# The last pair of row blocks: one sum turned, added and stored in two halves of rows

## The chip, the cores and the metric

The kernel runs on one core of a Trainium2 chip. Its time is the device time of one execution in microseconds (us); the figure of a kernel is the median of its runs. Five engines work side by side, each with its own queue: TensorE (PE in the profile; its weight loads are PEld), VectorE (DVE), ScalarE (ACT), GpSimd (POOL) and SyncE (SP), which only issues transfers. ScalarE issues transfers too (ACTq).

## The reference, cut to what matters

```
xn = layernorm(x)                              # x: 2048 rows, 640 columns
a, b = xn @ Wd_re.T, xn @ Wd_im.T              # DFT along the columns
y = Ws_re @ a - Ws_im @ b                      # DFT along the rows, real part
h = gelu(xn @ w1 + b1)                         # 640 -> 1536
out = x + y + (h @ w2 + b2)                    # 1536 -> 640
```

All inputs and the output are float32.

## The kernel before, in words

TensorE multiplies numbers split into a high and a low part, three matmuls for one product (`product`, `split`). First comes the GELU branch for four blocks of 512 rows, with x added; its results wait in DRAM (`ys`). Then the two Fourier products follow, the second as a fast product of seven multiplications, in which sums of operands replace multiplications.

The work after the GELU branch is a list of entries (w, u): w is one of the seven multiplications, u a part of it. Each entry has a *form*, an operand of TensorE in two halves: `form(n)` lets ScalarE write the high half (line 159) and VectorE the low half (line 160). The main loop goes through the entries in order. At entry n it emits TensorE's matmuls (`sequence_entry`, `hidden_entry`), then the functions listed as `pre` for that step, then `form(n + 3)`, then those listed as `post` (lines 1234 to 1238). So the lists fix VectorE's order by hand: what stands in `pre` runs ahead of the form, what stands in `post` behind it. Engines start their instructions in that order, and an instruction waits until the data that it needs is there and the place that it writes is free.

The stages named "y" (`hidden_beside`, `hidden_entry`) finish a pair of row blocks, ta and tb, over the hidden columns: 21 entries, w from 0 to 6 and u from 0 to 2. The results gather in PSUM banks. X, Y and Z stand for pairs of banks of 512 columns each (`banks[:, X : X + 2]` is `x_`), US and VS for single ones. A multiplication with w over 2 goes on in banks that an earlier one has begun. X is written by w = 0, 3, 5 and 6, and its contents are needed as they stand after w = 5, for block tb, and after w = 6, for block ta.

In the last pair (`last` is true), the matmuls of entries 18 to 20 (w = 6) are emitted at entries 18 and 19: at 18 first 15 into VS, which use the forms 18, 19 and 20 in turn, then 15 into bank X, and at 19 15 into bank X + 1 (from line 1188 on). These are TensorE's last 45 matmuls.

Step 17 is the one ahead of these. Its `pre` holds `add(v1, v1, x_)` on VectorE, then comes the last form, `form(20)`, and then `yb2, yb2`: the first call turns v1 in blocks of 32x32 (`turned`, line 839), the second adds what was turned to the columns 64 to 127 of each quarter of block tb (`columns(1)`, a tile that holds what the GELU branch left and was loaded into u2) and stores them (`out_b`, `store`). `add` is recorded as line 407, all issues of `store` as line 817. `store` issues four transfers, one for each quarter of the partitions; with `both` the first two go to SyncE's queue and the last two to ScalarE's. Step 18 does the same for VS (y4). After the loop, X is turned, added and stored (yt_2), and X + 1 in two halves of eight of the sixteen groups of rows (lines 1246 to 1257; yt_last).

A transfer signals its end through one of eight counters that the transfers of both queues take in rotation.

Of the kernel before, what the change touches and what calls it, by code (L numbers as in the profile page):

```python
# [17 lines left out]
B = 32  # L18
# [7 lines left out]
def kernel(  # L26
# [38 lines left out]
    nc = tc.nc  # L65
    x = x.flatten_outer_dims()
# [5 lines left out]
    NB = TB // B  # L72
# [32 lines left out]
    def bank(k):  # L105
        return banks[:, k]
# [62 lines left out]
    def rows_of(ap, t):  # L169
        return ap[t * TB : (t + 1) * TB].rearrange("(n r) d -> r n d", r=B)  # L170
# [108 lines left out]
    def hidden(g):  # L279
        i = g % NF  # L280
        acc = bank(g % 3)
        kinds = ((0, 0), (0, 1), (1, 0))
        steps = [(j, k) for j in range(ND) for k in range(3)]
        if g == 0:

            steps.sort(key=lambda s: s[1] == 1)
        for n, (j, k) in enumerate(steps):
            a, b = kinds[k]
            nc.tensor.matmul(  # L289
                acc, W1[i][:, a, j * P : (j + 1) * P], XT[j][:, b], start=n == 0, stop=n == len(steps) - 1  # L290
            )
        return acc
# [40 lines left out]
    A = {}  # L333
# [72 lines left out]
    def add(dst, a, b, op=ALU.add):  # L406
        nc.vector.tensor_tensor(dst, a, b, op=op)  # L407
# [23 lines left out]
    def load_a(g):  # L431

        for f in steps_of_load(g):
            f()
# [71 lines left out]
    def f5(u):  # L506
        add(held("ci1", u), held("ci1", u), held("ci2", u))

    def f6(u):
        add(held("cr1", u), held("cr1", u), held("ci1", u))  # L510
# [121 lines left out]
    last = NC - 1  # L632
# [91 lines left out]
    for g in range(NG):  # L724
# [9 lines left out]
        if i == NF - 1:  # L734
            acc = hidden(g + 2) if g + 2 < NG else None
# [19 lines left out]
        else:  # L755
            acc = hidden(g + 2)
# [42 lines left out]
    def load_part(t, k):  # L799
        nc.sync.dma_start(new_sum(1, t, k), part_of(t, k))  # L800

    def gather(h, t, k, acc, first=False, op=ALU.add):

        if h == 0 and first:
            nc.scalar.activation(new_sum(h, t, k), acc, AF.Copy, scale=-1.0 if op == ALU.subtract else 1.0)
        else:
            add(sums[t, k], sums[t, k], acc, op)
# [6 lines left out]
    def store(t, src, c0, c1, both=False, n0=0, n1=NB):  # L814

        for q in range(Q):
            (nc.scalar if both and q > 1 else nc.sync).dma_start(
                rows_of(out, t)[:, n0:n1, q * DQ + c0 : q * DQ + c1], src[q * B : (q + 1) * B, n0:n1]
            )
# [12 lines left out]
    def turned(acc, name):  # L832

        if len(acc.shape) == 2:
            yt = A["yt"](name)[:, 0]
            nc.vector.transpose(yt, acc)
        else:
            yt = A["yt"](name)
            nc.vector.transpose(yt.rearrange("p e n -> p (e n)"), acc.rearrange("p e n -> p (e n)"))
        return yt  # L840

    def add_turned(dst, yt):
        if len(yt.shape) == 2:
            add(dst, dst, yt.rearrange("p (n i) -> p n i", i=B))
        else:
            d = dst.rearrange("p n (e i) -> p e n i", i=B)
            add(d, d, yt.rearrange("p e (n i) -> p e n i", i=B))
# [182 lines left out]
    def load_g(b, i):  # L1030
        if i >= NW * ND:
            return
        w, c = G[i]
        n = GWIDE[w] * P
        places = A["g", b]
        k = i % len(places)
        if b < len(blocks) - 1 and w == NW - 1:

            k = (i - 2) % len(places)
            if c in CHUNKS[0]:  # L1040
                k = CHUNKS[0].index(c)
                places = {k: fr_tile((P, 6 * P), f"u{2 - k}_{sets[blocks[b]]}", f"gr{k}_{b}", F32R)}
        g = places[k][:, : 2 * n].rearrange("p (a b) -> p a b", a=2)
        GT[b, i] = g
        nc.sync.dma_start(g.bitcast(F32), wits[w][c])

    def hidden_beside(b, n):


        ta, tb = blocks[b - 1][1], blocks[b][1]  # L1050
        last = b == len(blocks) - 1
        x_, y_, z_ = (banks[:, k : k + 2] for k in (X, Y, Z))
        us, vs = bank(US), bank(VS)
        ya = yo[ta]

        def s(which, k):
            return sums[(ta, tb)[which], k]

        def t2(k):
            return lambda: add(s(1, KU[k]), s(1, KV[k]), s(1, KU[k]), ALU.subtract)  # L1060

        def t3(k):
            return lambda: add(s(0, KU[k]), s(1, KU[k]), s(0, KU[k]), ALU.subtract)

        def t4(k):
            return lambda: add(s(0, KV[k]), s(0, KV[k]), s(1, KU[k]), ALU.subtract)

        def columns(k):

            return s(1 if last else 0, ("u1", "u2")[k]).rearrange("p a b -> p (a b)").rearrange("p (n e) -> p n e", n=NB)  # L1070

        def load_yb(k):
            return lambda: nc.sync.dma_start(columns(k), ys[k][tb])

        def copy(dst, src):
            return lambda: nc.scalar.activation(dst, src, AF.Copy)

        def to(dst, acc, name, then=lambda: None):


            def f():
                add_turned(dst, turned(acc, name))
                then()

            return f

        def out_a(c0, c1):
            return lambda: store(ta, ya[:, :, c0:c1], c0, c1) if last else None

        def odd():  # L1090
            yt = turned(us, f"yo_{tb}")
            add_turned(ya[:, :, 4 * B :], yt)
            add_turned(yo[tb, 4], yt)
            out_a(4 * B, DQ)()

        def in_two(k):

            acc, name = s(1, ("v2", "v1")[k]), f"yb{k}_{tb}"

            def f():  # L1100
                if name not in A:
                    A[name] = turned(acc, name)
                else:
                    add_turned(columns(k), A.pop(name))
                    out_b(k)()

            return f

        def out_b(k):
            return lambda: store(tb, columns(k), 2 * k * B, 2 * (k + 1) * B, last and k == 1)  # L1110

        yb1, yb2 = in_two(0), in_two(1)
        yb4 = to(yo[tb, 4], vs, f"yb4_{tb}", lambda: store(tb, yo[tb, 4], 4 * B, DQ, last))
        f5s = [lambda u=u: f5(u) for u in range(2)] if not last else [lambda: None] * 2
        f6s = [lambda u=u: f6(u) for u in range(2)] if not last else [lambda: None] * 2
        pre = {
            17: [lambda: add(s(1, "v1"), s(1, "v1"), x_)],
        }.get(n, [])
        post = {

            0: [lambda: gather(1, tb, "v1", z_), lambda: gather(1, tb, "v", vs, op=ALU.subtract), f5s[0]],
            1: [f5s[1]],
            3: [to(ya[:, :, : 2 * B], x_, f"ya1_{ta}")],
            4: [t2(0)],
            5: [t2(1)],
            6: [to(ya[:, :, : 2 * B], y_, f"ya2_{ta}", out_a(0, 2 * B)), t2(2)],
            7: [odd],
            8: [t3(0)],
            9: [copy(s(1, "v1"), z_), t3(1)],
            10: [t3(2)],  # L1130
            11: [t4(0)],
            12: [copy(s(1, "v2"), x_), t4(1)],
            13: [load_yb(0), t4(2), load_yb(1)] if last else [t4(2)],
            14: [lambda: add(s(1, "v2"), s(1, "v2"), z_), yb1],
            15: [yb1] if last else [load_yb(0)],
            16: [] if last else [load_yb(1)],
            17: [yb2, yb2] if last else [yb1, yb2],
            18: [yb4] if last else [yb2],
            19: [f6s[0]],
            20: [] if last else [f6s[1], yb4],  # L1140
        }.get(n, [])
        if not last:
            if n in (12, 13):
                post.insert(0, lambda: load_g(b, (NW - 1) * ND + 13 - n))
            if n == 18:
                post[:0] = [lambda k=k: load_part(blocks[b + 1][1], k) for k in ("u1", "u")]
            if n == 20:
                post.append(lambda: load_a(put_off[0]))

                def end():  # L1150
                    to(ya[:, :, 2 * B : 4 * B], x_, f"ya3_{ta}")()
                    store(ta, ya, 0, DQ)

                later.append(end)
        return pre, post
# [91 lines left out]
    y = yo[t]  # L1247
    add_turned(y[:, :, 2 * B : 3 * B], turned(bank(X), "yt_2"))
    store(t, y[:, :, 2 * B : 3 * B], 2 * B, 3 * B, True)
    yt = A["yt"]("yt_last")[:, 0].rearrange("p (n i) -> p n i", i=B)  # L1250
    d, a = y[:, :, 3 * B : 4 * B], bank(X + 1).rearrange("p (n i) -> p n i", i=B)
# [36 lines left out]
```

## Time and profile before

| what | us |
|---|---|
| median of 3 runs | 862.92 (862.8 to 864.06) |
| the profiled execution | 862.76 |
| its span, first to last instruction | 861.0 |
| TensorE busy | 851.5 |
| VectorE busy | 623.4 |
| last matmul begins | 854.12 |
| last operation of VectorE ends | 856.27 |

The span starts at 0. The profile's timeline gives, for each instruction, its start, its duration, its engine, its line in the kernel, the tiles written and read, and in brackets how long the engine had been idle before it and what ended the wait. The view of waits sums these by who waited for whom. A transfer has an issue (the time on the queue that issues it) and a landing.

### The profile page before, as it was taken

The numbers are of one execution on the slowest core, as the hardware profiler recorded it, in microseconds if no ns is written. First come the engines' busy times: TensorE is split into PE (matmuls) and PEld (weight loads), VectorE is DVE, ScalarE is ACT, GpSimd is POOL, SyncE is SP. The second block draws the span as 40 slices with busy tenths as digits, with TensorE's granted clock in tenths as the row PEclk, the third lists the DMA queues.
The fourth block names the chain that finished last, engine by engine and source line by source line (L and its number), as shares of the span: only waits on it lengthen the run. The fifth ranks groups of instructions, "written<-read, shape, count | busy, mean of one in ns | idle before, by whom it ended". The sixth has DMA issues, their size and how long they took to land.

```text
span 861.0 us, 10245 instructions
## 1 busy us (share of the span) xinstructions
PE 851.5 (99%) x3754; PEld 703.4 (82%) x3754; DVE 623.4 (72%) x792; ACT 333.1 (39%) x460; POOL 21.0 (2%) x22
## 2 busy tenths in 40 slices
PE   8999999999999999999999999999999999999996
PEld 6888888888888888888888888888888888888885
DVE  6554555366443678989989787998977988885596
ACT  5454434245333555443434334232322423222241
POOL 0000300030003000000000000000000000000000
PEclk9999999999999999999999999999999999999999
DMA  6747476875566984938753659853765779704464
GB/s 180 226 134 180 89 183 182 215 157 174 155 164 152 321 357 88 221 103 213 173 145 86 184 172 278 209 132 101 196 175 167 257 181 230 304 19 177 126 186 86
DMA packets 208689, 152.34 MB, mean 177 GB/s; under 512 B 82432, under 2 KB 183040, under 8 KB 208128
## 3 DMA queue, kind: packets, MB, share of 16 engines
q1 hardware_dynamic: 195728, 137.93, 61.7%
q10 hardware_dynamic: 12912, 13.77, 4.6%
q8 instruction: 29, 0.48, 0.2%
q14 instruction: 20, 0.16, 0.1%
HBM read 108.67 MB, written 42.99 MB: 176 GB/s over the span
## 4 chain that ended last, share of the span: by engine, by line
PE 98%; DVE 1%; DMA 0%; ACT 0%; issue 0%
PE banks L272 26%; PE banks L273 26%; PE banks L271 26%; PE banks L289 19%; DMA x<-in_A_x_dram 0%; DVE st L184 0%; PE banks L627 0%; DVE yo L407 0%; DVE mv L185 0%; DVE yt_last L1254 0%; DVE xp L207 0%; ACT xt L159 0%; ACT mv L191 0%; DVE mv L193 0%; DVE mv L196 0%
## 5 line engine op out<-in xcount | busy, mean ns | idle before, releaser
L272 PE MATMUL banks<-as,xab 128*128 128x512 f32 x407 | 158.5, 389 | 0.0
L271 PE MATMUL banks<-as,xab 128*128 128x512 f32 x407 | 158.3, 389 | 0.0
L273 PE MATMUL banks<-as,xab 128*128 128x512 f32 x407 | 158.3, 389 | 0.0
L159 ACT ACTIVATE as<-r 128x1024 fp32r<-128x1024 f32 x80 | 85.0, 1062 | 173.6 <-PE banks L273 148.8
L160 DVE TENSOR_TENSOR as<-r,as 128x1024 fp32r<-128x1024 f32 x80 | 97.2, 1216 | 39.3 <-ACT as L159 39.3
L289 PE MATMUL banks<-xt,xab 128*128 128x512 f32 x420 | 99.2, 390 | 0.2 <-ACT xt L159 0.2
L304 DVE TENSOR_TENSOR hs<-ab,hs 128x512 fp32r<-128x512 f32 x48 | 36.5, 760 | 84.2 <-ACT hs L302 84.2
L289 PEld LDWEIGHTS banks<-xt,xab 128*128 128x128 f32 x420 | 78.4, 188 | 17.3 <-ACT xt L159 1.3
L272 PEld LDWEIGHTS banks<-as,xab 128*128 128x128 f32 x407 | 76.4, 188 | 16.5 <-DVE as L160 0.5
L271 PEld LDWEIGHTS banks<-as,xab 128*128 128x128 f32 x407 | 76.4, 188 | 15.9
L273 PEld LDWEIGHTS banks<-as,xab 128*128 128x128 f32 x407 | 76.4, 188 | 15.6
L271 PE MATMUL banks<-as,xc 128*128 128x512 f32 x224 | 87.1, 389 | 0.0
L272 PE MATMUL banks<-as,xc 128*128 128x512 f32 x224 | 87.1, 389 | 0.0
L273 PE MATMUL banks<-as,xc 128*128 128x512 f32 x224 | 87.1, 389 | 0.0
L298 ACT ACTIVATE ab<-banks,b1c 128x512 f32<-128x512 f32 x48 | 33.0, 688 | 100.6 <-PE banks L289 97.7
L159 ACT ACTIVATE as<-rt 128x1024 fp32r<-128x1024 f32 x32 | 34.0, 1062 | 70.1 <-PE banks L273 57.9
L289 PE MATMUL banks<-xt,as 128*128 128x512 f32 x240 | 57.0, 389 | 0.0
L289 PEld LDWEIGHTS banks<-xt,as 128*128 128x128 f32 x240 | 45.0, 188 | 9.4
L272 PEld LDWEIGHTS banks<-as,xc 128*128 128x128 f32 x224 | 42.0, 188 | 8.8
L271 PEld LDWEIGHTS banks<-as,xc 128*128 128x128 f32 x224 | 42.0, 188 | 8.8
L273 PEld LDWEIGHTS banks<-as,xc 128*128 128x128 f32 x224 | 42.0, 188 | 8.6
L271 PE MATMUL banks<-hs,xc 128*128 128x512 f32 x120 | 46.7, 389 | 0.0
(161 smaller groups left out, 1364.3 us busy)
## 6 DMA issues: line engine op xcount, KB each, us to landing
raw<-in_A_dft_seq_re_dram SPq DMA_DIRECT2D x64, 256.0 KB, 5.6
raw<-in_A_dft_seq_im_dram SPq DMA_DIRECT2D x64, 256.0 KB, 5.2
wit<-wst ACTq DMA_DIRECT2D x20, 384.0 KB, 3.5
ws<-wit SPq DMA_DIRECT2D x15, 384.0 KB, 5.2
xs<-x SPq DMA_DIRECT2D x64, 80.0 KB, 1.8
xo<-in_A_x_dram SPq DMA_DIRECT2D x16, 320.0 KB, 6.1
forms_ab<-xab SPq DMA_DIRECT2D x4, 1280.0 KB, 5.8
xab<-wit SPq DMA_DIRECT2D x13, 384.0 KB, 4.8
```

Of the source, the lines that this page charges most:

```text
L159: nc.scalar.activation(h, s, AF.Copy)
L160: nc.vector.tensor_tensor(l, s, h.bitcast(F32), op=ALU.subtract)
L271: nc.tensor.matmul(acc, wh, mh, start=first, stop=False, skip_group_check=goes_on)
L272: nc.tensor.matmul(acc, wh, ml, start=False, stop=False, skip_group_check=goes_on)
L273: nc.tensor.matmul(acc, wl, mh, start=False, stop=last, skip_group_check=goes_on)
L289: nc.tensor.matmul(acc, W1[i][:, a, j * P : (j + 1) * P], XT[j][:, b], start=n == 0, stop=n == len(steps) - 1)
L298: nc.scalar.activation(a, acc, AF.Gelu_apprx_tanh, bias=b1c[:, i : i + 1])
L304: nc.vector.tensor_tensor(hs[:, 1], a, hs[:, 0].bitcast(F32), op=ALU.subtract)
```

## The change

In the last pair, step 17 has no addition ahead of the last form any more. Behind the form, in place of the two calls of `yb2`, stands one new function, `by_halves`. For rows 0 to 7 of the sixteen groups, and then for rows 8 to 15, it adds the half of `x_` to the half of v1, turns that half, adds it to the half of `columns(1)`, and stores the half through both queues. `out_b` still serves the other stores, and its last argument is dropped. The other pair of row blocks keeps its order.

```diff
         def out_b(k):
-            return lambda: store(tb, columns(k), 2 * k * B, 2 * (k + 1) * B, last and k == 1)
+            return lambda: store(tb, columns(k), 2 * k * B, 2 * (k + 1) * B)
+
+        def by_halves():
+
+            acc, yt, d = s(1, "v1"), A["yt"](f"yb1_{tb}"), columns(1)
+            for n0 in (0, NB // 2):
+                n1 = n0 + NB // 2
+                a, x, y = (v[:, :, n0 * B : n1 * B] for v in (acc, x_, yt))
+                add(a, a, x)
+                nc.vector.transpose(y, a)
+                add_turned(d[:, n0:n1], y)
+                store(tb, d, 2 * B, 4 * B, True, n0, n1)
 
...
         pre = {
-            17: [lambda: add(s(1, "v1"), s(1, "v1"), x_)],
+            17: [] if last else [lambda: add(s(1, "v1"), s(1, "v1"), x_)],
         }.get(n, [])
...
-            17: [yb2, yb2] if last else [yb1, yb2],
+            17: [by_halves] if last else [yb1, yb2],
```

## The prediction

> **What bounds the kernel now.** First the page's table of engines (part 1) and its chain of work that ended last (part 4):
>
> ```profile
> PE 851.5 (99%) x3754; PEld 703.4 (82%) x3754; DVE 623.4 (72%) x792; ACT 333.1 (39%) x460; POOL 21.0 (2%) x22
> PE 98%; DVE 1%; DMA 0%; ACT 0%; issue 0%
> ```
>
> TensorE is busy for 99% of the span and makes up 98% of the chain. So an edit outside TensorE counts in two ways only: it makes TensorE wait or stop waiting, or it moves what follows TensorE's last matmul. The change touches VectorE's order and the stores at the very end, so I read two stretches of the timeline. The first is around the step that is edited, all engines (start, duration, engine, line, what it does):
>
> ```profile
> 845.06 1.22 DVE L407 TENSOR_TENSOR v<-v,banks 128x1024 f32<-128x1024 f32 x1
> ...
> 846.19 0.69 DVE L160 TENSOR_TENSOR as<-v,as 128x512 fp32r<-128x512 f32 x1
> ...
> 846.52 0.39 PE L271 MATMUL banks<-as,xab 128*128 128x512 f32 x1
> 846.79 1.24 DVE L839 STREAM_TRANSPOSE yb<-v 128x1024 f32<-128x1024 f32 x1
> 846.93 0.19 PEld L272 LDWEIGHTS banks<-as,xab 128*128 128x128 f32 x1 [0.45 <-DVE as L160]
> 846.93 0.50 PE L272 MATMUL banks<-as,xab 128*128 128x512 f32 x1
> ...
> 847.27 0.40 PE L273 MATMUL banks<-as,xab 128*128 128x512 f32 x1
> ...
> 847.50 0.40 PE L271 MATMUL banks<-as,xab 128*128 128x512 f32 x1
> ...
> 848.07 1.23 DVE L407 TENSOR_TENSOR u<-u,yb 128x1024 f32<-128x1024 f32 x1
> ```
>
> The first row is the full-width addition that step 17 runs ahead of the last form; the L160 row is the low half of that form; the transpose and the last row are yb2. The matmul at 846.93 is the first that needs the low half (ended 846.88). Matmuls start 0.227 us apart elsewhere, so it was due at 846.75: a wait of 0.19 us, then one spacing of 0.34 and ten that sum to about 0.05 too much. Eleven spacings on, TensorE is **0.34 us** late. No other VectorE wait holds TensorE after 840 us.
>
> The second stretch is the end, from the timelines of VectorE, ScalarE's queue and SyncE's queue, and the waits of SyncE's queue (total, times, longest):
>
> ```profile
> 855.85 0.43 DVE L407 TENSOR_TENSOR yo<-yo,yt_last 128x256 f32<-128x256 f32 x1
> ```
> ```profile
> 855.49 1.88 ACTq L817 DMA_DIRECT2D out_dram<-yo  x4
> ```
> ```profile
> 857.13 1.82 SPq L817 DMA_DIRECT2D out_dram<-yo  x4
> ```
> ```profile
> SPq L817 <- DMA out_dram<-yo: 2.7, 3, 1.4
> ```
>
> ScalarE issues its four last stores from 855.49, as soon as the data is there. SyncE issues its own four only from 857.13, since each transfer also waits for an earlier transfer to land. The trace's records of the transfers show why: each raises one of eight counters, taken in rotation through one list of the transfers of both queues, and waits until the transfer eight places earlier has landed. In the last part of the list ScalarE's stores stand ahead of SyncE's. SyncE's first store of the last half-block waits for ScalarE's store issued at 855.49, which lands 1.6 us later.
>
> **The change, part by part.** Times are those of the profiled execution: 862.76 us, of which 861.0 are the span and 1.76 lie around it; it is 0.16 under the median of 862.92, so the sum can stand beside the median.
>
> *The addition leaves its place ahead of the last form.* The L160 row moves from 846.19 to 845.06 (ScalarE's high half ended at 844.63) and ends at 845.75, ahead of the matmul due at 846.75. The wait goes: minus 0.34.
>
> *What is late next.* `by_halves` issues six operations in this order: add, turn, add turned for rows 0 to 7, then the same for rows 8 to 15. The two additions named `add(a, a, x)` read the banks X and X+1. Entry 18 (line 1192) first fills bank VS with 15 matmuls, and then writes X, starting over the same columns that the additions read. Before, one addition had read X by 846.28, over a microsecond before the first matmul into X (847.50, or 847.20 without the wait above). Now X is free only after the second half's addition, and that is fifth in VectorE's queue behind the low half. Durations: additions of 128x512 take 0.69, and start 0.60 after the one before when they need not wait for it (846.19 to 846.79); a transpose of 128x512 takes 0.72; an operation that needs the one before starts 0.03 after its end (848.07 against 846.79 + 1.24). So:
>
> - low half 845.06 to 845.75; first add 845.66 to 846.35; transpose 846.38 to 847.10; add of the turned half 847.13 to 847.82; second add 847.73 to **848.42**.
> - First matmul into X: 0.05 after that (846.88 to 846.93), at 848.47, instead of 847.20. Wait 1.27, and the 0.15 that the restart cost above (0.34 less 0.19): plus **1.42**.
>
> TensorE's end therefore moves by 1.42 − 0.34 = **+1.08**, from 854.51 to 855.59. The wait is not in the trace of before; its lower end is 0 (the additions released early, or the second half of the bank not protected) and its upper end 2.9, if all six operations had to end (849.89) ahead of X. I take 1.42, since only the two additions read X. Behind the waiting matmul stand 29 more, which all move with it, and behind these the last transposes. VectorE's other work is covered: its six halves end at 849.89 instead of 849.30, y4 then ends at about 851.4, and X is ready for the next transpose only at 852.2.
>
> The page "VectorE: DVE Perf Modes" of the Trainium skill, section "The DRAIN you can't avoid", says that the next operation does not start until the pipe of the one before is empty, except for those that need not be held. The rows show starts 0.09 us ahead of the end before; by the strict reading the second add would end at 848.69 and the forecast be 0.27 higher.
>
> *The stores.* Two stores of four transfers replace one: SyncE and ScalarE each issue two more, of 64 KB instead of 128. An issue takes 0.32 to 0.5 us, ScalarE has nothing else to do there, and SyncE's last ones come after the TensorE end anyway. What counts is whom the last SyncE transfers wait for. I carry the rotation on by hand: each queue's transfers are listed in the pace at which the list of before has them, half as long for 64 KB. Then SyncE's second store of the half X (the one named yt_2) falls eight behind ScalarE's first store of the last half-block, and four transfers stand behind it; before, it was the next one, with three behind it. With everything 1.08 later: ScalarE's store is issued at 856.57, has landed by 858.2, and five SyncE issues follow at 0.45 each (1.82 for four): the last at 860.0, landed 1.65 later (these stores' medians are 1.6 and 1.7). Before, the last was issued at 858.5. So the tail adds **+0.45**. Ends: the gate one place further back, 0; one or two places ahead, +0.9 or +1.35; no gate at all, about −2.2 (last add at 857.36, two issues, landing at 859.45 instead of 861.67).
>
> Sum: 862.76 + 1.08 + 0.45 = **864.3 us**.
>
> **Rivals.**
>
> - *No new wait, the old one gone.* If X were free in time (both additions run first, or nothing ties the second to X), TensorE gains 0.34: 862.4, or 862.9 with the tail's 0.45. Against it: the written order, and that bank X is continued, not started anew. 10%.
> - *The stores' queue, slower than forecast and slower than before.* The place is SyncE's queue after 857; it decides if ScalarE's store that is late stands eight ahead of a SyncE transfer with six or more instead of four behind it: 0.45 for each, so 865.2 to 865.6. For it: ScalarE gets two more transfers ahead and SyncE already lags 2 us. 17%.
> - *The rotation falls well.* SyncE's last stores then wait for nothing late: 864.3 − 2.2 = 862.1 with the new wait; near 860.6 only if the new wait fails to come too. 6%, of which 2 for the latter.
> - *The clock.* The longer wait could lower TensorE's granted clock. The nearest row is the stretch after TensorE stops, with a clock of 0.73; 30 matmuls at 0.227 would take 9.3 instead of 6.8 us: 866.8. The clock stayed at 1.00 through the old wait. 3%. The Trainium skill's page "TensorE: Matmul & The Clock Gate", section "HAM oscillation — how this bites in real kernels", names idle gaps over about 3.4 us as the cause; no run here has a gap of 1.3 us to show it.
>
> **How the numbers follow.** The forecast has 64%, between 863.4 and 864.9. A measurement of this kernel can tell about 0.2%, or 1.7 us: faster means below 861.2, slower above 864.65. Of the forecast's 64 some 14 lie above 864.65. Slower: 14 + 17 + 3 = 34%. Faster: the 2% where the rotation falls well and the wait does not come, and one more for what I overlook: 3%. Within 0.2%: 63%. The range takes the forecast, most of the first rival and of the stores' queue: 862.2 to 865.5.
>
> **What would show it.** In the profile after: the L160 row of 128x512 at about 845.1 and no wait of TensorE for it; a TensorE wait of 1.2 to 1.3 us near 847.2, put down to VectorE's L407, at the first matmul of a new bank; the last matmul's end near 855.6; SyncE's late store issued some 1.6 us after ScalarE's first store of the last half-block, and four more behind it. Wrong would be: a last matmul at 854.2 (no new wait), or a last store that lands less than 5 us after it (the rotation fell well).

## The result, and the profile after

| | before | changed |
|---|---|---|
| median, 13 runs of each | 862.8 us | 865.1 us |
| profiled execution | 862.76 | 865.58 |
| its span | 861.0 | 863.8 |
| last 45 matmuls, first start to last start | 10.32 | 11.39 |
| start of the last matmul to the last landing | 6.02 | 6.78 |
| last landing to the end of the span | 0.83 | 1.08 |

The changed kernel is slower: ratio 1.0025, 95% interval 1.0017 to 1.0032, or +2.2 us (1.5 to 2.8). The last three rows of the table, read from the starts and landings in the two traces, add up to +2.07. The remaining 0.7 of the two profiles' difference lies ahead of the edited step: the group of 45 starts 0.71 later, in code that is the same in both. The profiles of the experiments have this shift between −0.2 and +0.3 (+0.1 in two that hold the halved block too, sums_first and one_store), and the profiled execution is the longest of the changed kernel's 13, 0.48 over their median. So I put the shift down to the execution and not to the change; what makes it is not shown. One run of an experiment below, quarters, took 1075.3 us at a mean granted clock of 0.75 and is left out of that kernel's figures.

The page's parts 1 and 4 of the changed kernel:

```profile
PE 852.7 (99%) x3754; PEld 703.9 (81%) x3754; DVE 624.0 (72%) x795; ACT 333.4 (39%) x460; POOL 21.0 (2%) x22
PE 96%; DVE 2%; DMA 1%; ACT 0%; issue 0%; ACTq 0%
```

TensorE is still the bound. VectorE has three operations more, and its share of the chain goes from 1% to 2%. Where it gained is in the timeline around step 17 of the changed kernel (times are about 0.7 later than in the profile before, as said):

```profile
844.64 1.82 DVE L160 TENSOR_TENSOR as<-v,as 128x1024 fp32r<-128x1024 f32 x2
...
846.38 0.68 DVE L407 TENSOR_TENSOR v<-v,banks 128x512 f32<-128x512 f32 x1
...
847.10 0.71 DVE L1119 STREAM_TRANSPOSE yb<-v 128x512 f32<-128x512 f32 x1
847.26 0.40 PE L271 MATMUL banks<-as,xab 128*128 128x512 f32 x1
847.50 0.39 PE L272 MATMUL banks<-as,xab 128*128 128x512 f32 x1
847.73 0.40 PE L273 MATMUL banks<-as,xab 128*128 128x512 f32 x1
847.85 0.69 DVE L407 TENSOR_TENSOR u<-u,yb 128x512 f32<-128x512 f32 x1
848.46 0.68 DVE L407 TENSOR_TENSOR v<-v,banks 128x512 f32<-128x512 f32 x1
...
849.19 0.50 PE L271 MATMUL banks<-as,xab 128*128 128x512 f32 x1 [1.06 <-DVE v L407]
849.53 0.39 PE L272 MATMUL banks<-as,xab 128*128 128x512 f32 x1
```

The first row holds two low halves, those of the last two forms, and the last is done by 846.5. The matmuls at 847.26, 847.50 and 847.73 are those of the last form, and the one at 847.50 (line 272) reads this low half. They run at their spacing of 0.23: the old wait is gone. The next matmul, the first into X, was due at 847.96 and starts at 849.19, right behind the second addition (848.46 + 0.68 = 849.14). The bracket counts 1.06, from the end of the matmul before; by starts the delay is 1.23.

The waits of all engines in the changed kernel from 843 us (total, times, longest) say the same; the row of before, `PEld banks L272 <- DVE as L160`, is gone:

```profile
PEld banks L271 <- DVE v L407: 1.5, 1, 1.5
PE banks L271 <- DVE v L407: 1.1, 1, 1.1
```

At the end, ScalarE's and SyncE's last issues in the changed kernel:

```profile
857.27 1.87 ACTq L817 DMA_DIRECT2D out_dram<-yo  x4
```
```profile
859.04 2.41 SPq L817 DMA_DIRECT2D out_dram<-yo  x5
```

ScalarE issues 1.37 after the last matmul begins, as before (855.49 against 854.12). Its first store lands at 859.02, and at 859.04 SyncE goes on with five transfers; before, it went on with four (857.13, x4).

### The profile page after: what moved, and what is told of

The parts are those of the page before. It is cut to its first block, busy times and chain, and to the rows that moved or that the text cites. A ratio compares the mean times of both kernels' runs of the same rounds, so it can differ in the third digit from the quotient of the medians.

```text
span 863.8 us, 10254 instructions
## 1 busy us (share of the span) xinstructions
PE 852.7 (99%) x3754; PEld 703.9 (81%) x3754; DVE 624.0 (72%) x795; ACT 333.4 (39%) x460; POOL 21.0 (2%) x22
## 4 chain that ended last, share of the span: by engine, by line
PE 96%; DVE 2%; DMA 1%; ACT 0%; issue 0%; ACTq 0%
PE banks L271 26%; PE banks L272 26%; PE banks L273 26%; PE banks L289 19%; DMA w1r<-in_B_w_dram 1%; DVE as L160 1%; DVE v L407 0%; PE banks L627 0%; DVE u L407 0%; ACT as L159 0%; ACTq L177 0%; DVE yo L407 0%; DVE yt_last L1265 0%; DVE yb L1119 0%; DVE xp L207 0%
## 5 line engine op out<-in xcount | busy, mean ns | idle before, releaser
L272 PE MATMUL banks<-as,xab 128*128 128x512 f32 x407 | 158.3, 389 | 0.0
L160 DVE TENSOR_TENSOR as<-r,as 128x1024 fp32r<-128x1024 f32 x80 | 97.2, 1216 | 39.1 <-ACT as L159 39.1
L272 PEld LDWEIGHTS banks<-as,xab 128*128 128x128 f32 x407 | 76.4, 188 | 16.0
L272 PE MATMUL banks<-as,xc 128*128 128x512 f32 x224 | 87.1, 389 | 0.0
L272 PEld LDWEIGHTS banks<-as,xc 128*128 128x128 f32 x224 | 42.0, 188 | 8.7
```

The costliest lines, as they stand in the source:

```text
L160: nc.vector.tensor_tensor(l, s, h.bitcast(F32), op=ALU.subtract)
L272: nc.tensor.matmul(acc, wh, ml, start=False, stop=False, skip_group_check=goes_on)
```

## The experiments

Ten kernels were run beside the kernel before (its median is 862.87 to 862.9 in all three groups of runs). "45" are the last 45 matmuls, "end" the time from the start of the last matmul to the last landing, "close" what follows the landing.

| run | 45 | end | close | median | ratio to before (95%) |
|---|---|---|---|---|---|
| before | 10.32 | 6.02 | 0.83 | 862.9 | |
| changed | 11.39 | 6.78 | 1.08 | 865.1 | 1.0025 (1.0017 to 1.0032) |
| whole_behind | 10.03 | 6.57 | 0.83 | 863.12 | 1.0003 (0.9995 to 1.0012) |
| sums_first | 10.03 | 6.51 | 1.08 | 863.42 | 1.0008 (1.0000 to 1.0017) |
| one_store | 11.39 | 6.20 | 0.83 | 864.17 | 1.0016 (1.0007 to 1.0025) |
| half_stores | 10.31 | 6.32 | 1.08 | 863.65 | 1.0010 (1.0001 to 1.0019) |
| sum_third | 10.65 | 6.87 | 1.09 | 864.51 | 1.0018 (1.0009 to 1.0027) |
| before_both | 13.79 | 4.63 | 0.89 | 863.86 | 1.0015 (1.0006 to 1.0024) |
| even_queues | 9.99 | 4.61 | 0.89 | 861.18 | 0.9981 (0.9973 to 0.9990) |
| halves_even_queues | 11.42 | 4.63 | 1.13 | 862.79 | 0.9998 (0.9990 to 1.0007) |
| even_only | 10.30 | 4.63 | 0.89 | 861.59 | 0.9986 (0.9977 to 0.9995) |
| quarters | 14.45 | 5.75 | 0.83 | 866.4 | 1.0035 (1.0023 to 1.0047) |

The intervals are as wide as many of the steps, so the medians only confirm sums; the readings rest on the profiles, one execution of each kernel.

### The addition behind the form, in one piece

```diff
-            17: [lambda: add(s(1, "v1"), s(1, "v1"), x_)],
+            17: [] if last else [lambda: add(s(1, "v1"), s(1, "v1"), x_)],
...
-            17: [yb2, yb2] if last else [yb1, yb2],
+            17: [lambda: add(s(1, "v1"), s(1, "v1"), x_), yb2, yb2] if last else [yb1, yb2],
```

> The whole addition (128x1024, 1.22 us) stands behind the last form and ahead of the transpose; nothing is halved. Theory (TensorE's wait is that of bank X for the fifth operation in VectorE's queue): the addition ends at about 846.9 on the clock of the profile before, ahead of the first matmul into X at 847.20, so TensorE waits for nothing, its last matmul comes 0.34 us earlier than before, the stores' end is as before (6.0 us from the start of the last matmul to the last landing), and the time is about 0.3 us under before, too little for the comparison. Rival (the addition behind the form is what costs, halved or not): TensorE waits 0.7 us or more for X, and the time is 0.5 us or more above before.

The waits of this kernel from 843 us hold no row of TensorE any more:

```profile
ACT as L159 <- PE banks L273: 1.9, 2, 1.7
DVE yt_last L1254 <- PE banks L273: 1.7, 1, 1.7
```

The 45 matmuls take 10.03, 0.29 less than before, so moving the addition is not what costs. The expectation missed the end: it grew by 0.55, and the time is not under before. Its last issues:

```profile
855.18 1.87 ACTq L817 DMA_DIRECT2D out_dram<-yo  x4
```
```profile
857.26 1.93 SPq L817 DMA_DIRECT2D out_dram<-yo  x4
```

ScalarE issues 0.30 earlier than before, but SyncE goes on 0.13 later (857.26 against 857.13): the store that it waits for took 2.01 to land instead of 1.58, and the next one 2.33. What TensorE gained was lost between the queues.

### Both half sums first

```diff
+            parts = []
             for n0 in (0, NB // 2):
...
                 add(a, a, x)
+                parts.append((n0, n1, a, y))
+            for n0, n1, a, y in parts:
                 nc.vector.transpose(y, a)
                 add_turned(d[:, n0:n1], y)
...
```

> As the changed kernel, but both half additions run first, then turn, add and store half by half. Theory: the second addition ends at about 846.95, TensorE does not wait for X, and its last matmul comes 0.34 us earlier than before, 1.4 us earlier than in the changed kernel; the stores are listed as in the changed kernel, so the end stays 0.75 us longer from the last matmul to the last landing, and some 0.25 us longer behind that; together +0.5 to +0.7 us over before. Rival (the waiting is not the additions' but that of all six operations): TensorE still waits 1.2 us or more, and the time stays at +2.1 us.

Against the changed kernel only the order of the six operations differs. TensorE has no wait for VectorE left, and the 45 matmuls fall from 11.39 to 10.03: the whole wait was the place of the second addition. What remains over before is the stores' part, −0.29 + 0.49 + 0.25 = +0.45 by the profile, +0.55 by the medians.

### One store for both halves

```diff
-                store(tb, d, 2 * B, 4 * B, True, n0, n1)
+            store(tb, d, 2 * B, 4 * B, True)
```

> As the changed kernel, but the two halves are stored by one store of four transfers at the end, as before. Theory: TensorE's wait of about 1.2 us for X stays, last matmul +1.07 us over before; the rotation of the counters is back to that of before, SyncE's first held store is again the first of the last half-block, the stores' end is 6.0 us, the time +1.1 us. Rival (the stores cost nothing, the rest of the slowdown is noise of the start): no difference from the changed kernel beyond 0.2 us.

The last 45 matmuls take 11.39 again (the wait by starts is 1.28, in the changed kernel 1.23), and the end and the close come down to 6.20 and 0.83. The end is not quite the 6.0 expected: ScalarE's store that SyncE waits for took 1.76 to land, in the kernel before 1.58. Profile: +1.07 + 0.17 = +1.24 over before; medians: +1.30.

### Two half stores alone

```diff
+            if last and k == 1:
+                return lambda: [
+                    store(tb, columns(k), 2 * k * B, 2 * (k + 1) * B, True, n0, n0 + NB // 2) for n0 in (0, NB // 2)
+                ]
...
```

> The kernel before with one edit: the store of the second pair of columns is issued as two stores of half the rows behind one another, eight transfers in place of four. Theory (not the number of transfers counts, but whom the last ones wait for): here SyncE's first store of the last half-block waits again for ScalarE's, with three behind it, so the stores' end is 6.0 us as before and the time within 0.2 us of before. Rival (four more transfers lengthen the end by their number): the stores' end is 6.75 us and the time 0.75 to 1.0 us above before.

Neither theory as stated. SyncE's late issues in this kernel:

```profile
857.39 1.82 SPq L817 DMA_DIRECT2D out_dram<-yo  x4
```

Four of them come behind the gate (the landing of ScalarE's store that SyncE waits for), as the rotation gives, and not five. Still the end is 6.32: the store at the gate landed 1.86 after its issue, 0.28 more than before. And the close grew to 1.08. The profile is +0.54 over before; the medians give +0.78, which is the rival's time, but its end of 6.75 did not come. After the last landing SyncE asks the counters one after another; with 600 transfers in all, the last one uses the counter that is asked last, with 604 it uses one that is asked earlier, and four more questions of 0.06 follow. All kernels with 604 transfers have 1.08 to 1.13 there, all with 600 have 0.83 to 0.89.

### The second sum one place earlier

```diff
+            (a0, x0, y0), (a1, x1, y1) = half
+            add(a0, a0, x0)
+            nc.vector.transpose(y0, a0)
+            add(a1, a1, x1)
+            add_turned(d[:, : NB // 2], y0)
...
```

> As the changed kernel, but the second half addition is moved one operation forward: first sum, first transpose, second sum, then the rest. Theory (TensorE waits until the second addition ends): that end comes one operation earlier, at about 847.7 on the clock of the profile before, and the first matmul into X, due at 847.20, waits 0.55 us instead of 1.23; with 0.1 for the restart the last 45 matmuls take 10.03 + 0.65 = 10.7 us (before 10.32, changed 11.39). The stores are listed as in the changed kernel. Time: about +1.4 us over before. Rival (TensorE's wait depends on something else in the halved block, say the transpose or the store): the 45 matmuls take 11.4 us, or 10.0.

The first matmul into X starts right behind the second addition, which ended at 847.99:

```profile
848.05 0.50 PE L271 MATMUL banks<-as,xab 128*128 128x512 f32 x1 [0.31 <-DVE v L407]
```

A dose between the two: it comes 0.70 after the matmul before it, a wait of 0.48 by starts, and the 45 matmuls take 10.65. Predicted were 0.55 and 10.7. The profile's parts give +0.33 + 0.84 + 0.26 = +1.43 over before, as expected; the medians give +1.61.

### The first pair's store through both queues

```diff
-            return lambda: store(tb, columns(k), 2 * k * B, 2 * (k + 1) * B, last and k == 1)
+            return lambda: store(tb, columns(k), 2 * k * B, 2 * (k + 1) * B, last)
```

> The kernel before, with one edit: the store of the first pair of columns goes through both queues too, two transfers on each, instead of four on SyncE's. The transfers of both queues then stand alternately in the list from there on, and no transfer of SyncE's waits for a late one of ScalarE's. Theory (the end is set by whom SyncE's last transfers wait for): SyncE issues its stores of the last half-block from about 855.5 instead of 857.1, the last landing comes 4.4 to 4.7 us after the last matmul begins instead of 6.0, the 45 matmuls stay at 10.3, and the time is 1.3 to 1.6 us under before. Rival (the end is set by the transfers' own pace, and the waits only look like it): the end stays within 0.3 us of 6.0.

The end is 4.63, as expected: SyncE's last transfers wait for no late one of ScalarE's. But the time is not under before: the median is 1 us over it, and the profiled execution, one of the longer (864.94), is 2.2 over it, because its 45 matmuls take 13.79. The waits from 843 us:

```profile
PE banks L271 <- ACT as L159: 0.9, 1, 0.9
PE banks L272 <- DVE as L160: 0.8, 1, 0.8
```

Step 15 put two store issues into ScalarE's queue ahead of the high halves of the last two forms:

```profile
844.09 0.95 ACTq L817 DMA_DIRECT2D out_dram<-u  x2
845.13 1.58 ACT L159 ACTIVATE as<-v 128x1024 fp32r<-128x1024 f32 x2 [4.11 <-issue]
```

The issues wait for VectorE until 844.09, and the forms behind them come 2.5 and 2.1 us late (842.64 and 844.00 before). TensorE waits twice for 1.04 us, and then the granted clock falls. The stretches of this kernel follow (us; busy by engine; the last three numbers are the granted clock, the DMA share and GB/s):

```profile
846.00:848.00 2.00, 1.00 (x3) 0.63 (x4) 1.77 (x2) 0.71 (x2) 0.00 (x0) 1.00 0.64 141
848.00:850.00 2.00, 2.00 (x8) 1.48 (x7) 2.00 (x3) 0.00 (x0) 0.00 (x0) 0.59 0.00 0
850.00:852.00 2.00, 2.00 (x7) 1.56 (x6) 1.86 (x3) 0.00 (x0) 0.00 (x0) 0.56 0.00 0
852.00:854.00 2.00, 2.00 (x10) 1.66 (x9) 1.11 (x2) 0.00 (x0) 0.00 (x0) 1.00 0.81 189
```

Between 848.7 and 851.7 the matmuls start 0.43 apart instead of 0.23. The nine spacings from 848.32 to 851.97 sum to 3.65 instead of 2.04, so the clock costs 1.6 us here. By the times it did not fall in every run: four of the 11 runs took 864.9 to 865.2 us, at a mean granted clock of 0.997, and the other seven 863.4 to 864.1, at 0.999. In these seven the two waits alone would account for the longer time; no profile shows one of them.

### Both edits, with ScalarE's stores behind the form

The whole addition behind the last form, as in whole_behind, and the first pair's store through both queues. Its two transfers on ScalarE's queue are issued in step 17, behind the last form (the diff is cut):

```diff
...
-            17: [yb2, yb2] if last else [yb1, yb2],
+            17: [lambda: add(s(1, "v1"), s(1, "v1"), x_), other_quarters, yb2, yb2] if last else [yb1, yb2],
...
+            if last and k == 0:
+                return lambda: store(tb, columns(k), 2 * k * B, 2 * (k + 1) * B, True, quarters=(0, 1))
...
+        def other_quarters():
+            store(tb, columns(0), 0, 2 * B, True, quarters=(2, 3))
```

> The whole addition behind the last form, and the first pair's store through both queues, ScalarE's two transfers of it behind the last form so that they don't delay its high half. Theory: TensorE's last 45 matmuls take 10.03 us, the stores' end is 4.4 to 4.7 us, the time 1.6 to 1.9 us under before, the fastest of all. Rival (what TensorE gains is lost again in the stores, as where the whole addition alone was moved): the stores' end is 0.3 longer than with the queues alone and the time equal to that one.

This is the fastest kernel, 1.7 us under before. SyncE's last four stores start at 855.19, with ScalarE's (855.19 too), and not 1.6 us behind them as before:

```profile
855.19 1.80 SPq L817 DMA_DIRECT2D out_dram<-yo  x4
```

### The changed kernel with even queues

The changed kernel with the same edit to the first pair's store.

> The changed kernel with the first pair's store through both queues, ScalarE's part of it behind the last form. Theory (two separate causes, TensorE's wait for X and the stores' end): the wait stays, 45 matmuls take 11.4 us, the stores' end is 4.4 to 4.7 us, with 0.25 behind the last landing as in the changed kernel; the time is between 0.2 us under and 0.2 us over before, some 2 us under the changed kernel. Rival (the halved stores themselves take longer): the stores' end is over 5.2 us and the time over +0.6 us.

The wait for X is all there (11.42), and the end is 4.63: the two causes are separate and add. The halves cost TensorE 1.10 us and the close 0.30, which the better end (1.39) just pays back.

### Even queues alone

The kernel before, addition ahead of the form, with the same edit to the first pair's store.

> The kernel before with the first pair's store through both queues, ScalarE's part behind the last form; the addition stays ahead of the form. Theory (the miss of before_both was ScalarE's queue, where two store issues that waited for data stood ahead of two forms): the 45 matmuls take 10.3 us again, the stores' end is 4.6 us, the time 1.3 to 1.5 us under before. Against the run with the whole addition moved as well it shows whether TensorE's 0.3 us comes through once the stores no longer wait: then this kernel is 0.3 us slower than that one. Rival: the two are equal.

TensorE's old wait is back (10.30) and the end is that of the last two kernels. Beside even_queues the profiles differ by the 0.31 of TensorE alone, and the medians by 0.41 (their intervals overlap): with the queues even, what TensorE gains reaches the end.

### Quarters

```diff
-            for n0 in (0, NB // 2):
-                n1 = n0 + NB // 2
+            for n0 in range(0, NB, NB // 4):
+                n1 = n0 + NB // 4
...
-                store(tb, d, 2 * B, 4 * B, True, n0, n1)
+            store(tb, d, 2 * B, 4 * B, True)
```

> The changed kernel's block in four quarters of rows instead of two halves, with one store at the end. Theory (TensorE waits for the last addition that reads X): that is now the tenth operation, at 0.42 to 0.45 us each; it ends at 849.9 on the clock of before, the wait is 2.7 us instead of 1.23, the 45 matmuls take 12.9 us if the granted clock holds, the time is 2.6 to 3.0 us over before. Rival (a longer wait also lowers the granted clock, as two waits of 1.05 us did in before_both): about ten matmuls at 0.43 us spacing instead of 0.23, 45 matmuls in 14.7 us, time 4.4 to 4.8 us over before.

The wait is 2.70 by starts, as worked out from the tenth operation, and in the profiled execution the clock fell behind it, as the rival has it:

```profile
849.70 0.76 PE L271 MATMUL banks<-as,xab 128*128 128x512 f32 x1 [2.54 <-DVE v L407]
850.26 0.63 PE L272 MATMUL banks<-as,xab 128*128 128x512 f32 x1
850.69 0.63 PE L273 MATMUL banks<-as,xab 128*128 128x512 f32 x1
851.12 0.63 PE L271 MATMUL banks<-as,xab 128*128 128x512 f32 x1
```

The next eight matmuls start 0.41 to 0.56 apart, and the stretches show the granted clock (third number from the end):

```profile
848.00:850.00 2.00, 0.30 (x1) 0.30 (x2) 1.90 (x6) 0.00 (x0) 0.00 (x0) 0.94 0.00 0
850.00:852.00 2.00, 2.00 (x6) 1.54 (x6) 1.83 (x4) 0.00 (x0) 0.00 (x0) 0.50 0.20 51
852.00:854.00 2.00, 2.00 (x8) 1.61 (x7) 0.14 (x1) 0.00 (x0) 0.00 (x0) 0.71 1.33 253
```

Three runs took 866.4 to 866.8 us, at a mean granted clock of 0.996 to 0.997, and two 865.1, at 0.999 and 1.000. The profile is one at 866.4. The mean clocks fit that the clock held in the two at 865.1, but no profile of one shows it. Against before these are +3.5 to +4.0 and +2.2 us, each under what its theory gave (4.4 to 4.8 and 2.6 to 3.0).

## Why the prediction was right, and where it was short

- **The old wait goes.** Forecast −0.34; the runs without any wait show 10.32 − 10.03 = −0.29. Right but for 0.05: the ten spacings that are 0.05 too long together, which I counted to the wait, stand in whole_behind too (845.38 to 847.47), where TensorE waits for nothing. The price of the restart is the first spacing, 0.34 instead of 0.23.
- **What is late next: bank X behind the fifth operation.** Forecast: wait 1.27, TensorE's end +1.08. Measured: 1.23 and 11.39 − 10.32 = +1.07. That the sum agrees to 0.01 is partly luck: it was 1.42 − 0.34 and came out as 1.36 − 0.29. That the second addition does it is shown by four places of the last addition among the operations of the block: second (sums_first: no wait), third (0.48), fourth (1.23), and tenth, in quarters (2.70). The upper end of 2.9, that all six operations count, is out.
- **Operations overlap by 0.09 when they need not wait.** The strict reading of "The DRAIN you can't avoid" (page "VectorE: DVE Perf Modes" of the Trainium skill) gave 0.27 more. In the changed kernel the second addition starts at 848.46, 0.08 ahead of the end of the one before (847.85 + 0.69): the rows, and the section's own exception, hold.
- **The clock.** It held behind the wait of 1.23: 1.00 in the stretches from 847 to 853 of the profile after, and the 13 runs lie within 0.9 us, with no group 1.6 above the others. The Trainium skill's page "TensorE: Matmul & The Clock Gate", section "HAM oscillation — how this bites in real kernels", names TensorE-idle gaps of more than about 3.4 us as what lowers the clock; the changed kernel agrees with it. Two experiments do not, and there the measurement decides: in the profiles of quarters and before_both the clock fell behind one wait of 2.70 and behind two of 1.04 close together. So the rival's mechanism is real. That the wait of the changed kernel was too short for it fits, but the limit was not looked for.
- **The stores: the term that was mis-sized.** The place was right: SyncE's second store of yt_2 waits for ScalarE's first of the last half-block, and four follow. Forecast +0.45; measured 0.75 up to the last landing, and 0.25 behind it that I had not thought of. The 0.75 are: the issues behind the gate 1.96 instead of 1.37 (+0.59; I had 1.80, but the next transfer waits for ScalarE's second store, which landed at 859.59); the store at the gate 1.76 instead of 1.58 to its landing (+0.18); the rest −0.02. I took one duration, 1.6, for a landing that the runs show between 1.55 and 2.0 (the next store, issued 0.4 later, took 2.33 in whole_behind); what sets it stays open. The 0.25 are the closing questions to the counters.

So the sum was 1.53 and the measured parts are 2.07. The sign and both mechanisms hold and the time lies in the range, but the likeliest side (within 0.2%) was the wrong one, by half a microsecond in the stores.

## What to carry to other kernels

When a reader of a bank is split in pieces, look at who writes the bank next: it waits for the last piece that reads, wherever the queue has it, so let all pieces that read it run first. Before you shorten the work ahead of the last stores, read whom each last transfer waits for: counters that both queues take in rotation can tie one queue's stores to the other's latest, and here evening out the queues was worth over four times the edit of the compute (1.3 us against 0.3). An issue that waits for data holds up everything behind it on its engine; put it behind the work that TensorE needs.

## What the runs showed of the hardware that was not expected

- The granted clock can fall behind short waits: in the kept profiles it did not behind one of 1.23, but it did behind one of 2.70 and behind two of 1.04 with one matmul between them. In both it was at half for 3.4 us, worked out from the stretches (their clocks are 0.06 + 0.50 + 0.29 and 0.41 + 0.44 short of 1.00, over 2 us each), and cost about 1.6 us. The length of the wait alone does not seem to decide: by their times and mean clocks, runs of the same kernel differ (three of five of quarters, four of 11 of before_both fell). What else decides was not tried.
- After a wait of 0.19, 0.48 or 1.23 the first spacing of the matmuls is 0.34 instead of 0.23. The ten or so spacings of up to 0.24 that often follow are not the wait's: whole_behind and sums_first have ten of them, from 845.4 and 845.5 on, with no wait of TensorE. What makes them is open.
- A 32 KB store took from 1.5 to 2.3 us from issue to landing. What sets it was not tried.
